# Attention and spectral mixing on one core: weight subtractions on GpSimd, earlier block loads, later rounding

## The chip, the cores and the metric

The kernel runs on one core of a Trainium2 chip. The metric is the device time of one execution in microseconds (us); lower is better. Engines are named as in the profile: PE is TensorE (PEld its weight loads), DVE is VectorE, ACT is ScalarE, POOL is GpSimd and SP is SyncE, which issues nearly all DMAs here.

## The reference

The input x has 2048 rows of 512. Two branches are mixed by a gate that each row computes for itself:

```python
x = A_x
g = _sigmoid((x * gate_w).sum(-1, keepdims=True))
a = _A_ref(x, A_wqkv, A_wo)      # attention, 32 heads of 16, softmax over 2048 keys, then @ wo
b = _B_ref(x, ...)               # y = Cr @ (x @ Wr.T) - Ci @ (x @ Wi.T): real part of a 2-D DFT
return g * a + (1 - g) * b
```

All of it is in 32-bit floats.

## The kernel before

**Matmuls in three passes.** TensorE multiplies a rounded type (F32R). To keep precision, each operand is split into a rounded part hi and a remainder lo = raw - hi. ScalarE makes hi by a copy with a change of type, and VectorE or GpSimd subtracts to make lo. A product is then hi x hi + hi x lo + lo x hi. The two halves of 64 rows run beside each other into two PSUM banks, so one pass is one pair of matmuls. This pair is the unit of the kernel's own calendar: `slots` counts pairs, and `beside()` is called after each.

**The calendar.** `after(n, f, ...)` puts a step into the instruction streams n slots from now. It sets only the place of the step in the order of its engine's queue. Each engine takes its queue in order, and an instruction that waits holds up all behind it on its engine.

**The stages.** In the first 680 us the kernel makes queries and keys (`project_t`, 12 slots each), values and the two DFT products of x (`project_s`, 12 slots each), and then the DFT along the sequence over blocks of 128 rows (48 slots each). Beside these it scans: matmuls of queries with keys, of which only the row maxima are kept (`scan`, and from a certain point `scan_folded`, which needs a ScalarE copy named fold and a VectorE maximum named fold or mx for each pair of chunks). How often a scan is placed between the pairs is set in slots (`scan_at`). After 680 us the attention itself follows, with exponentials on ScalarE.

**The steps that the change touches:**

- `project_t`: when a projection's 24 matmuls are done, ScalarE copies one bank to tx (one buffer), VectorE or GpSimd adds the other bank into s (three buffers), ScalarE rounds s into eh and GpSimd subtracts to make el; both are stored. The banks serve the projection after next.
- The weights of queries (wq) and keys (wk) come in two column halves, near and far. Splits of the far halves are placed by `after`: `split_w` is one ScalarE copy and one subtraction for each of the four row blocks d. The far halves of wq are first read by the projection that begins at slot 144.
- `project_s`: ScalarE copies one bank (tx, L545); the other is copied to ty (one buffer) or read directly; an add into va (values) or ab (DFT) follows on GpSimd or VectorE.
- `gate_sums` begins with the fourth block of the values. 16 blocks of x are loaded by SyncE into two buffers in turn, multiplied by the gate weights on GpSimd (`weigh`) and halved by adds (`add_up`); `gates` finishes the sum, and z, g = 1 / (1 + exp(-sum)) and gm = 1 - g follow. EVERY is 24 slots.
- `fold_keys`: key blocks are loaded, GpSimd subtracts one from another (fa), ScalarE rounds the difference (fh) and GpSimd makes the remainder; both are stored for later scans. It is called four times in the first DFT product.
- `renew`: in the DFT along the sequence the 16 right operands (second operands, b tiles) are exchanged when the cosine part is done. ScalarE rounds each, and four slots later GpSimd (odd) or VectorE (even) subtracts.

Of the kernel before, what the change touches and what calls it, by code (L numbers as in the profile page):

```python
# [10 lines left out]
F32 = mybir.dt.float32  # L11
F32R = mybir.dt.float32r
AF = mybir.ActivationFunctionType
ALU = mybir.AluOpType
# [10 lines left out]
NB = S // P  # L25
# [29 lines left out]
EVERY = 24  # L55
# [13 lines left out]
def build(tc, xT, xr, wqkv, wo, wrT, wiT, cr, ci, ct, gate, out):  # L69
    nc = tc.nc  # L70
    with ExitStack() as ctx:
# [25 lines left out]
        z = keep.tile([P, NB], F32, name="z")  # L97
        g = keep.tile([P, NB], F32, name="g")
        gm = keep.tile([P, NB], F32, name="gm")
# [103 lines left out]
        def halves_of(ps, lhs, rhs, first, last):  # L203

            for j in range(2):
                r = slice(64 * j, 64 * j + 64)
                nc.tensor.matmul(ps[j], lhs[r], rhs[r], start=first, stop=last)  # L207
# [65 lines left out]
        with ExitStack() as pf:  # L273
# [31 lines left out]
            def after(n, f, *args):  # L305

                count[0] += 1
                due.append((slots[0] + n, count[0], f, args))
# [21 lines left out]
            def beside():  # L330

                slots[0] += 1
                run_due()
                if pace[0] is None:
                    return
                since = slots[0] - spare[1] + 10
                pace[1] += 1.0 / (pace[0] if pace[0] != PART or since > 48 else CALM if since <= 8 else KEEN)
                while seen[0] < FRONT and pace[1] >= 1.0:
                    pace[1] -= 1.0
                    n = seen[0]  # L340
                    if n == FOLDED.start:
                        begin_folds()
                    if n in ROWS:
                        load_scan_beside(ROWS[n])
                    if n not in FOLDED:
                        scan(n, s1())
                        done = n
                    else:

                        scan_folded(n, 0, *beds)  # L350
                        done = behind(n - 1)
                    seen[0] += 1
                    if seen[0] == FRONT:
                        done = behind(n)
                    if done is not None and SEQ[done][1] == SCANS - 1:
                        for d, part in enumerate(shift(SEQ[done][0], nc.scalar.copy, nc.gpsimd.tensor_sub)):
                            maxima.append(part)
                            after((3, 8, 26, 31, 36)[d], part)
# [66 lines left out]
            with ExitStack() as px:  # L425
# [7 lines left out]
                def new_w():  # L433
                    ts = [wb.tile([P, ND, 512], F32R, tag=f"w{i}", name=f"w{i}") for i in range(2)]
                    return [[t[:, d, :] for d in range(ND)] for t in ts]

                def new_cw():

                    return list(zip(*(coefficients() for d in range(ND))))
# [14 lines left out]
                def fold_keys(f, g):  # L454

                    a, b = (ep.tile([P, 512], F32, tag="el", name="fa", bufs=4) for _ in range(2))
                    c = 2 * g
                    parts = [(a, b)]
                    if f:
                        for i, v in enumerate((a, b)):  # L460
                            nc.sync.dma_start(v, ks_d[f][:, (c + i) * 512:(c + i + 1) * 512])
                    else:

                        parts.append([rp.tile([P, 512], F32, tag="raw", name="fl") for _ in range(2)])
                        for n in range(2):
                            for i in range(2):
                                nc.sync.dma_start(parts[n][i], k_d[f][:, n, (c + i) * 512:(c + i + 1) * 512])
                        nc.sync.dma_start(kf_d[f][:, :, (c + 1) * 512:(c + 2) * 512],
                                          k_d[f][:, :, (c + 1) * 512:(c + 2) * 512])
                    hi = ep.tile([P, 512], F32R, tag="gb", name="fh", bufs=1)  # L470
                    lo = b.bitcast(F32R)

                    def store(i, v):
                        nc.sync.dma_start(kf_d[f][:, i, c * 512:(c + 1) * 512], v.bitcast(F32))

                    wait = 0 if f else 26
                    after(14 + wait // 2, nc.gpsimd.tensor_sub, a, a, b)
                    if wait:
                        after(33, nc.gpsimd.tensor_sub, parts[1][0], *parts[1])
                        after(39, nc.gpsimd.tensor_add, a, a, parts[1][0])  # L480
                    after(wait + 22, nc.scalar.copy, hi, a)
                    after(wait + 24, nc.gpsimd.tensor_sub, lo, a, hi.bitcast(F32))
                    after(wait + 28, store, 0, hi)
                    after(wait + 31, store, 1, lo)

                kept = []

# [66 lines left out]
                wq, wk = new_w(), new_cw()  # L554
                raws = [stk.tile([P, S], F32, tag="stk", name="raws") for _ in range(6)]
                q4 = [slice(d * 512, (d + 1) * 512) for d in range(4)]
                rq, rk = ([raws[4 + i][:, q4[d]] for d in range(ND)] for i in range(2))
                near, far = slice(0, 256), slice(256, 512)
# [24 lines left out]
                    split_w(wq, d, rq[d], cols=near)  # L583
                for d in range(ND):
                    after(1 + 2 * d, split_w, wk, d, rk[d], nc.vector, near)
                    after(84 + 5 * d, split_w, wq, d, rq[d], nc.vector, far)
                    after(130 + 12 * d, split_w, wk, d, rk[d], nc.vector, far)
                    for c in range(1, NC):
                        after(24 * c - 6 + 4 * d, split_x, d, c)
                def gate_sums():  # L590

                    work = stk.tile([P, 4, D], F32, tag="stk", name="gated")
                    sums_ = work[:, 3, :].rearrange("p (t k) -> p t k", k=32)
                    nc.sync.dma_start(work[:, 0, :], gate.to_broadcast([P, D]))

                    def load(t):
                        nc.sync.dma_start(work[:, 1 + t % 2, :], xr[t])

                    def weigh(t):
                        v = work[:, 1 + t % 2, :]  # L600
                        nc.gpsimd.tensor_mul(v, v, work[:, 0, :])

                    def add_up(t):
                        v = work[:, 1 + t % 2, :]
                        for n in (256, 128, 64):
                            nc.gpsimd.tensor_add(v[:, 0:n], v[:, 0:n], v[:, n:2 * n])
                        nc.gpsimd.tensor_add(sums_[:, t, :], v[:, 0:32], v[:, 32:64])

                    for t in range(NB):
                        after(EVERY * t, load, t)  # L610
                        after(EVERY * t + 22, weigh, t)
                        after(EVERY * t + 34, add_up, t)
                    after(EVERY * NB + 22, gates, sums_)

                def gates(sums_):
                    for n in (16, 8, 4, 2):
                        nc.gpsimd.tensor_add(sums_[:, :, 0:n], sums_[:, :, 0:n], sums_[:, :, n:2 * n])
                    nc.gpsimd.tensor_add(z, sums_[:, :, 0], sums_[:, :, 1])
                    after(10, lambda: nc.scalar.activation(z, z, AF.Exp, scale=-1.0))

                    def rest():
                        nc.vector.tensor_scalar_add(z, z, 1.0)
                        nc.vector.reciprocal(g, z)
                        nc.vector.tensor_scalar(gm, g, -1.0, 1.0, op0=ALU.mult, op1=ALU.add)

                    after(14, rest)

                order = [(wq, q_d, 0, 0), (wk, k_d, 0, 0), (wq, q_d, 1, 0)]
                order += [(w, dst, 0, c) for c in range(1, NC) for w, dst in ((wq, q_d), (wk, k_d))]
# [37 lines left out]
                for n, wait in enumerate((18, 78, 152, 202)):  # L667
                    after(wait, fold_keys, 2 * (n // 2), n % 2)
# [20 lines left out]
            with ExitStack() as py:  # L689
# [36 lines left out]
                for n, (ph, t, u) in enumerate(coef):  # L726
# [12 lines left out]
                    hi, lo = ready.pop(n)  # L739
# [25 lines left out]
                    for w in range(CS):  # L765
                        s = u * CS + w
                        for i, (c_, a_) in enumerate(((hi, ah[s]), (hi, al[s]), (lo, ah[s]))):
                            halves_of(pss[t], c_[:, w, :], a_, s == 0 and i == 0, s == NB - 1 and i == 2)
                            beside()
                            if n >= len(coef) - NU and 3 * s + i in AHEAD:  # L770
                                go_ahead(AHEAD.index(3 * s + i))
                        if swap:
                            if 3 <= s < 8:
                                early[s + 5] = load_operand(1, s + 5, cp)
                            after(1 + 5 * (s % 8) + 4 * (s // 8), renew, s)
                    if u == NU - 1:
                        tx = cp.tile([P, D], F32, tag="tx", name="tx")
                        last = n == len(coef) - 1
# [18 lines left out]
        with ExitStack() as pa:  # L797
# [143 lines left out]
            parts = []  # L941
# [435 lines left out]
```

## Time and profile before

| | us |
|---|---|
| median of 3 runs | 1709.04 |
| lowest and highest | 1708.09, 1710.79 |
| profiled execution | 1709.94 |
| its span, first to last instruction | 1708.0 |
| PE busy | 1691.4 |
| ACT busy | 1499.2 |
| DVE busy | 1189.2 |
| POOL busy | 818.9 |

Times in the views are us from the start of the span. A line of the order of time has start, duration, engine, line, operation, written tile <- read tiles, shapes, count, and in brackets the idle time just before it and what ended it. Lines such as L320 are shared by all steps that `after` or a helper places, so the names of the tiles tell which step it is. Busy time of PE is modelled from pipelined matmuls. PEclk is the granted clock as a share of the full one.

### The profile page before, as it was taken

The page shows a single profiled execution, that of the slowest core. Times are in us where ns is not written, and L with a number is a line of the kernel's source. Part 1 is how long each engine was busy: PE and PEld are TensorE (multiplying, and loading weights), DVE is VectorE, ACT ScalarE, POOL GpSimd, SP SyncE. Part 2 cuts the span into 40 slices and gives each one's busy share as a digit, 9 for nine tenths or more (in the row PEclk, how much of TensorE's full clock was granted, in tenths as well). Part 3 has the DMA queues.
Part 4 walks back from the last instruction along what each step waited for, and adds up shares of the span by engine and source line. Part 5 has one row for each costly group of instructions (what it writes and reads, how often), then busy time and mean ns, then how long its engine had stood idle before and what let it go on. Part 6 is the DMA issues. An engine that isn't in the chain of part 4 may idle for free.

```text
span 1708.0 us, 36306 instructions
## 1 busy us (share of the span) xinstructions
PE 1691.4 (99%) x13524; PEld 1036.1 (61%) x13524; DVE 1189.2 (70%) x2171; ACT 1499.2 (88%) x2470; POOL 818.9 (48%) x998
## 2 busy tenths in 40 slices
PE   9999999999999999999999999999999999999998
PEld 7898888889899895333333333333345555555554
DVE  5898888899999896666676666666742456653343
ACT  5447888888888888999999999999998888888886
POOL 3577676755556861434545455352323333334222
PEclk9999999999999999999999999999999999999999
DMA  7684668544448764355445445353426465575833
GB/s 263 237 286 116 215 200 223 168 120 126 119 126 216 195 136 95 100 138 133 134 115 123 109 127 141 82 148 63 101 67 145 139 149 151 135 187 139 196 90 127
DMA packets 151584, 251.18 MB, mean 147 GB/s; under 512 B 49792, under 2 KB 60528, under 8 KB 144112
## 3 DMA queue, kind: packets, MB, share of 16 engines
q1 hardware_dynamic: 136144, 227.49, 49.1%
q0 software_dynamic: 14688, 20.33, 5.1%
q8 instruction: 106, 1.74, 0.5%
q10 hardware_dynamic: 576, 1.05, 0.2%
q14 instruction: 70, 0.57, 0.1%
HBM read 168.56 MB, written 81.01 MB: 146 GB/s over the span
## 4 chain that ended last, share of the span: by engine, by line
PE 89%; DMA 2%; POOL 1%; DVE 1%; issue 1%; SPq 0%; ACT 0%; DVEq 0%; POOLq 0%; ACTq 0%
PE pvb L822 28%; PE xy L207 20%; PE s L232 19%; PE s L176 9%; PE s L207 8%; PE s L157 4%; DMA gated<-xr 1%; DVE fold L182 0%; DMA k_d<-eh 0%; DMA kf_d<-eh 0%; DVE y L937 0%; SPq L923 0%; DMA b<-o_d 0%; POOL va L648 0%; POOL el L320 0%
## 5 line engine op out<-in xcount | busy, mean ns | idle before, releaser
L256 ACT ACTIVATE eb<-s 128x1024 f32<-128x1024 f32 x512 | 579.3, 1132 | 60.2 <-PE s L232 60.1
L264 ACT ACTIVATE e<-s 128x512 f32<-128x512 f32 x1022 | 609.7, 710 | 0.0
L159 DVE TENSOR_REDUCE mx<-s 128x2 f32<-128x1024 f32 x380 | 460.9, 1224 | 195.7 <-PE s L157 195.5
L822 PE MATMUL pvb<-eb,va 128*17 128x512 f32 x2052 | 514.4, 597 | 0.0
L822 PE MATMUL pvb<-e,va 128*17 128x512 f32 x2044 | 513.5, 597 | 0.0
L182 DVE CUSTOM_DVE_ANT_0 fold<-s,fold 128x512 f32<-128x512 f32 x644 | 434.5, 690 | 53.1 <-PE s L176 29.4
L180 ACT ACTIVATE fold<-s 128x512 f32<-128x512 f32 x644 | 383.9, 602 | 66.3 <-PE s L176 37.7
L232 PEld LDWEIGHTS s<-qs,ks 50*128 50x128 f32 x2048 | 214.0, 184 | 361.6 <-ACT eb L256 268.7
L232 PE MATMUL s<-qs,ks 50*128 50x512 f32 x2048 | 424.3, 436 | 0.0
L207 PE MATMUL xy<-b,c 64*128 64x512 f32 x2448 | 382.6, 391 | 0.2 <-ACT c L376 0.2
L176 PE MATMUL s<-ks,qs 64*128 64x512 f32 x1288 | 283.8, 395 | 4.6 <-DVE mx L182 2.1
L207 PEld LDWEIGHTS xy<-b,c 64*128 64x128 f32 x2448 | 267.2, 184 | 23.5 <-ACT c L376 0.5
L822 PEld LDWEIGHTS pvb<-eb,va 128*17 128x17 f32 x2052 | 69.8, 96 | 189.5 <-issue 180.2
L176 PEld LDWEIGHTS s<-ks,qs 64*128 64x128 f32 x1288 | 149.5, 184 | 32.4 <-DVE mx L182 10.8
L157 PE MATMUL s<-ks,qs 48*128 48x512 f32 x760 | 160.3, 395 | 0.0
L841 POOL DMA_DIRECT2D r_d<-lc x31 | 18.0, 580 | 274.9 <-DVE lc L840 227.0
L207 PE MATMUL s<-b,b 64*128 64x512 f32 x1050 | 136.4, 390 | 0.2 <-DMA b<-o_d 0.2
L207 PE MATMUL xy<-w,b 64*128 64x512 f32 x768 | 116.6, 391 | 0.0
L834 POOL DMA_DIRECT2D lc<-ob x124 | 63.0, 515 | 109.6 <-DVE ob L831 104.6
L207 PEld LDWEIGHTS s<-b,b 64*128 64x128 f32 x1050 | 99.7, 185 | 24.1 <-issue 1.0
L408 POOL TENSOR_TENSOR c<-craw,c 128x512 fp32r<-128x512 f32 x84 | 109.9, 1309 | 6.7
L843 POOL DMA_DIRECT2D rb<-r_d x124 | 60.5, 495 | 96.1 <-DMA r_d<-lc 92.2
(147 smaller groups left out, 1624.8 us busy)
## 6 DMA issues: line engine op xcount, KB each, us to landing
qs<-q_d SPq DMA_DIRECT2D x90, 256.0 KB
craw<-cr SPq DMA_DIRECT2D x60, 256.0 KB
craw<-ct SPq DMA_DIRECT2D x48, 256.0 KB
ks<-k_d SPq DMA_DIRECT2D x46, 256.0 KB
ks<-kf_d SPq DMA_DIRECT2D x44, 256.0 KB
kept_None<-sum SPq DMA_DIRECT2D x40, 256.0 KB
craw<-kept_None SPq DMA_DIRECT2D x40, 256.0 KB
craw<-ci SPq DMA_DIRECT2D x32, 256.0 KB
```

The costliest lines, as they stand in the source:

```text
L157: nc.tensor.matmul(ps[:, j, :], qs[b:b + 48, qb * P:(qb + 1) * P], ks[b:b + 48, c * 512:(c + 1) * 512], start=True, stop=True)
L159: nc.vector.tensor_reduce(mx[p][:, :, qb, c], ps, axis=AX.X, op=ALU.max)
L176: nc.tensor.matmul(ps, qs[b:b + 64, qb * P:(qb + 1) * P], ks[b:b + 64, c * 512:(c + 1) * 512], start=True, stop=True)
L180: nc.scalar.activation(fold[j], ps, AF.Relu)
L182: nc.vector.tensor_tensor_reduce(out=fold[j], in0=ps, in1=fold[j], scale=1.0, scalar=-3.0e38, op0=ALU.add, op1=ALU.max, accum_out=mx[p][:, ...
L207: nc.tensor.matmul(ps[j], lhs[r], rhs[r], start=first, stop=last)
L232: nc.tensor.matmul(pss[j], ks[b:b + 50, kb * P:(kb + 1) * P], qs[b:b + 50, q0:q0 + 512], start=True, stop=True)
L256: nc.scalar.activation(e, ps, AF.Exp, scale=SCALE)
L264: nc.scalar.activation(e[j], pss[j], AF.Exp, scale=SCALE)
L408: sub(lo, raw, hi.bitcast(F32))
L822: nc.tensor.matmul(pvb[r:r + VC, :], va[:, kb, 2 * p + j, :], es[c][j], start=kb == 0, stop=kb == NB - 1, tile_position=(0, r))
L834: nc.gpsimd.dma_start(lc[32 * n:32 * n + 32, :], ob[r + DH:r + VC, :].rearrange("p (s e) -> p s e", e=16))
```

## The change

```diff
-                    after(wait + 22, nc.scalar.copy, hi, a)
-                    after(wait + 24, nc.gpsimd.tensor_sub, lo, a, hi.bitcast(F32))
-                    after(wait + 28, store, 0, hi)
-                    after(wait + 31, store, 1, lo)
+                    after(wait + 30, nc.scalar.copy, hi, a)
+                    after(wait + 32, nc.gpsimd.tensor_sub, lo, a, hi.bitcast(F32))
+                    after(wait + 36, store, 0, hi)
+                    after(wait + 40, store, 1, lo)
...
-                    after(84 + 5 * d, split_w, wq, d, rq[d], nc.vector, far)
+                    after(106 + 10 * d, split_w, wq, d, rq[d], nc.gpsimd, far)
...
-                        after(EVERY * t, load, t)
-                        after(EVERY * t + 22, weigh, t)
-                        after(EVERY * t + 34, add_up, t)
-                    after(EVERY * NB + 22, gates, sums_)
+                        at = EVERY * t + 40
+                        after(at - 35 if t > 1 else 0, load, t)
+                        after(at, weigh, t)
+                        after(at + 8, add_up, t, 256)
+                        after(at + 12, add_up, t, 128, 64, 32)
+                    after(EVERY * NB + 30, gates, sums_)
...
                     after(10, lambda: nc.scalar.activation(z, z, AF.Exp, scale=-1.0))
-                        nc.vector.tensor_scalar_add(z, z, 1.0)
-                        nc.vector.reciprocal(g, z)
-                        nc.vector.tensor_scalar(gm, g, -1.0, 1.0, op0=ALU.mult, op1=ALU.add)
-                    after(14, rest)
+                    after(16, nc.gpsimd.tensor_scalar_add, z, z, 1.0)
+                    after(24, nc.vector.reciprocal, g, z)
+                    after(30, lambda: nc.gpsimd.tensor_scalar(gm, g, -1.0, 1.0, op0=ALU.mult, op1=ALU.add))
...
-                            after(1 + 5 * (s % 8) + 4 * (s // 8), renew, s)
+                            after(1 + 5 * (s % 8) + 14 * (s // 8), renew, s)
```

1. `fold_keys`: the rounding fh comes 8 slots later, the remainder too, the stores 8 and 9 slots later.
2. The four splits of wq's far halves come at slots 106, 116, 126 and 136 instead of 84, 89, 94 and 99, with the subtraction on GpSimd instead of VectorE.
3. Block t of x is loaded at slot 24t + 5 from the third block on (24t before), multiplied at 24t + 40 (24t + 22), and its sum is taken in two pieces at 24t + 48 and 24t + 52 (24t + 34 in one). Its buffer was freed by the sum of block t - 2, now at 24t + 4, before at 24t - 14.
4. `gates` begins at slot 414 instead of 406. The addition of 1 and gm move to GpSimd; the reciprocal stays on VectorE, and the three come 16, 24 and 30 slots after the sums instead of 14 for all.
5. `renew` of operands 8 to 15 comes 10 slots later.

TensorE's instructions stay the same and in the same order. Line numbers behind the gate's functions fall by two.

VectorE in the projections, around 30 us of the profile. The w rows are the far halves of wq, b is a part of x, s the sums of a projection's two banks, and c a far half of wk:

```order
 L320 TENSOR_TENSOR s<-xy,tx 128x512
 L377 TENSOR_TENSOR b_236<-raws,b_235 128x512
-L377 TENSOR_TENSOR w_238<-raws,w_237 128x256 x2
 L320 TENSOR_TENSOR s<-s_544,tx 128x512
-L377 TENSOR_TENSOR w_238<-raws,w_237 128x256 x2
 L320 TENSOR_TENSOR s<-xy,tx 128x512 x3
 L377 TENSOR_TENSOR c<-raws,c 128x256
```

The four subtractions ahead of two adds are gone; the adds follow each other. On GpSimd the four now stand one by one between subtractions that make el.

ScalarE at the third call of `fold_keys`, around 231 us; tx and ty are copies of `project_s`, w a split of the next weights. Before:

```order
L376 CAST w_2701<-wraw 128x512
L180 ACTIVATE fold<-s 128x512 x2
L545 ACTIVATE tx<-xy 128x512
L180 ACTIVATE fold<-s 128x512 x2
L320 CAST fh<-fa 128x512
L180 ACTIVATE fold<-s 128x512 x3
L545 ACTIVATE tx<-xy 128x512
```

and now:

```order
L376 CAST w_2696<-wraw 128x512
L180 ACTIVATE fold<-s 128x512 x2
L545 ACTIVATE tx<-xy 128x512
L180 ACTIVATE fold<-s 128x512 x5
L545 ACTIVATE tx<-xy 128x512
L320 CAST fh<-fa 128x512
L180 ACTIVATE fold<-s 128x512 x4
```

The rounding fh stands three folds and one tx later.

More of the change, by code (lines that the diff above doesn't have):

```diff
@@ L601, in weigh, with add_up @@
                         nc.gpsimd.tensor_mul(v, v, work[:, 0, :])
-                    def add_up(t):
+                    def add_up(t, *parts):
                         v = work[:, 1 + t % 2, :]
-                        for n in (256, 128, 64):
-                            nc.gpsimd.tensor_add(v[:, 0:n], v[:, 0:n], v[:, n:2 * n])
-                        nc.gpsimd.tensor_add(sums_[:, t, :], v[:, 0:32], v[:, 32:64])
+                        for n in parts:
+                            dst = sums_[:, t, :] if n == 32 else v[:, 0:n]
+                            nc.gpsimd.tensor_add(dst, v[:, 0:n], v[:, n:2 * n])
                     for t in range(NB):
-                        after(EVERY * t, load, t)
-                        after(EVERY * t + 22, weigh, t)
-                        after(EVERY * t + 34, add_up, t)
-                    after(EVERY * NB + 22, gates, sums_)
+                        at = EVERY * t + 40
[4 more added lines that the diff above has]
+                    after(EVERY * NB + 30, gates, sums_)
                 def gates(sums_):
@@ L619, in gates @@
                     after(10, lambda: nc.scalar.activation(z, z, AF.Exp, scale=-1.0))
-                    def rest():
-                        nc.vector.tensor_scalar_add(z, z, 1.0)
-                        nc.vector.reciprocal(g, z)
-                        nc.vector.tensor_scalar(gm, g, -1.0, 1.0, op0=ALU.mult, op1=ALU.add)
-                    after(14, rest)
+                    after(16, nc.gpsimd.tensor_scalar_add, z, z, 1.0)
+                    after(24, nc.vector.reciprocal, g, z)
+                    after(30, lambda: nc.gpsimd.tensor_scalar(gm, g, -1.0, 1.0, op0=ALU.mult, op1=ALU.add))
                 order = [(wq, q_d, 0, 0), (wk, k_d, 0, 0), (wq, q_d, 1, 0)]
```

## The prediction

> **What bounds the kernel now.** I read the page's totals first, then the waits of TensorE, then its busy time in stretches of 10 us, and at each stretch that falls short the instructions in order of time.
>
> ```profile
> span 1708.0 us, 36306 instructions
> PE 1691.4 (99%) x13524; PEld 1036.1 (61%) x13524; DVE 1189.2 (70%) x2171; ACT 1499.2 (88%) x2470; POOL 818.9 (48%) x998
> PE s L176 <- DVE mx L182: 2.1, 6, 0.5
> PE s L176 <- ACT fold L180: 2.0, 2, 1.3
> PE xy L207 <- DVE s L320: 1.3, 1, 1.3
> PE xy L207 <- ACT tx L516: 0.6, 1, 0.6
> ```
>
> TensorE is busy 99% of the span, and the change leaves its instructions as they are, in number and order. So only two things can move the time: where TensorE stands still, and its clock. What it can win is a few microseconds of stalls; what it can lose is a new stall wherever a moved instruction is late. The four wait rows (total, times, longest) already name the places; the stretches date them:
>
> ```profile
> 120.00:130.00 10.00, 10.00 (x90) 9.81 (x88) 10.00 (x10) 2.85 (x7) 4.02 (x4) 1.00 1.04 344
> 130.00:140.00 10.00, 8.89 (x72) 7.00 (x70) 7.06 (x13) 5.43 (x11) 5.75 (x8) 1.00 0.29 84
> 230.00:240.00 10.00, 8.66 (x75) 7.39 (x74) 7.45 (x22) 7.35 (x14) 6.87 (x10) 1.00 0.65 200
> 260.00:270.00 10.00, 9.49 (x82) 7.79 (x80) 8.97 (x27) 8.64 (x19) 5.27 (x5) 1.00 0.47 142
> 550.00:560.00 10.00, 9.19 (x73) 6.79 (x73) 9.06 (x23) 8.54 (x17) 8.94 (x9) 1.00 0.72 185
> 37.00:41.00 4.00, 4.00 (x24) 0.57 0.65 248
> ```
>
> The columns are the stretch, its length, the busy time of PE, PEld, DVE, ACT and POOL, the granted clock, DMA share and GB/s (the last row, asked for PE alone, has PE's). An undisturbed stretch has 10.00 and some 90 matmuls. Short are 130 to 140 by 1.1 us, 230 to 240 by 1.3, 260 to 270 by 0.5, 550 to 560 by 0.8; and from 37 to 41 the granted clock is 0.57. Each lies where one edit works.
>
> **Far halves of the query weights (VectorE to GpSimd, later).** This is the largest term.
>
> ```profile
> 29.26 0.62 ACT L320 CAST eh<-s 128x512 fp32r<-128x512 f32 x1 [1.11 <-DVE s L320]
> 30.09 0.58 ACT L516 COPY tx<-s 128x512 f32<-128x512 f32 x1
> 30.22 1.65 DVE L377 TENSOR_TENSOR w<-raws,w 128x256 fp32r<-128x256 f32 x2 [0.39 <-ACT w L376]
> 30.45 2.90 PE L207 MATMUL xy<-b,c 64*128 64x512 f32 x24
> 31.80 0.68 DVE L320 TENSOR_TENSOR s<-s,tx 128x512 f32<-128x512 f32 x1
> 33.34 0.58 ACT L516 COPY tx<-xy 128x512 f32<-128x512 f32 x1
> 33.47 1.62 DVE L377 TENSOR_TENSOR w<-raws,w 128x256 fp32r<-128x256 f32 x2 [0.99 <-ACT w L376]
> 33.97 0.50 PE L207 MATMUL xy<-b,w 64*128 64x512 f32 x1 [0.62 <-ACT tx L516]
> 35.01 0.68 DVE L320 TENSOR_TENSOR s<-xy,tx 128x512 f32<-128x512 f32 x1
> 35.75 6.45 PE L207 MATMUL xy<-b,w 64*128 64x512 f32 x40 [1.28 <-DVE s L320]
> 42.98 0.59 ACT L516 COPY tx<-xy 128x512 f32<-128x512 f32 x1 [0.92 <-PE xy L207]
> 45.70 0.59 ACT L516 COPY tx<-xy 128x512 f32<-128x512 f32 x1 [0.40 <-PE xy L207]
> ```
>
> A projection's banks come free in two steps: ScalarE copies one (tx), VectorE adds the other (s). TensorE waits 0.62 us for a copy and 1.28 us for an add. Both are late because of the four subtractions: the copy at 30.09 is done at 30.67, but its add starts at 31.80, behind two of them (30.22 to 31.87); the next copy is done at 33.92 and its add starts at 35.01, behind the other two. tx has a single buffer, so a late add delays the next copy too.
>
> What it costs now: the group at 30.45 ends at 33.35. Two projections later, undisturbed, the copy would start 2 x 2.72 us on (45.70 less 42.98 is the period), at 38.8. It starts at 42.98, so 4.1 us are lost: 1.9 of named waiting, 0.5 for a lone matmul between them, and 4 us at clock 0.57, worth 1.7.
>
> Without the subtractions, and with their casts behind the copies in ScalarE's queue: cast eh ends at 29.88, copy to 30.5, add to 31.3 (0.68 each add, a little for each hand-over), cast to 31.9, copy to 32.5, add to 33.3. TensorE wants the bank at 33.2 to 33.35. What is late next is this same add, by 0.1 or 0.2 us. I take 3.9 us gained, of 4.1 at most; the other end is 0, if casts and copies still collide. With the idle time gone I expect the slow stretch gone; if it stays, 2.4 are gained.
>
> On GpSimd:
>
> ```profile
> L320 POOL TENSOR_TENSOR el<-s,eh 128x512 fp32r<-128x512 f32 x32 | 41.3, 1289 | 38.3 <-ACT eh L320 38.0 <-POOL el L320 0.2
> L377 DVE TENSOR_TENSOR w<-raws,w x8: 410/418/1317, 5.1 to 34.7; 128x256 fp32r<-128x256 f32 x8
> ```
>
> Half as wide as el, a subtraction there costs between half of 1.29 us and all of it; I take 0.7. One el and one subtraction per 2.72 us fit, since GpSimd waits 38.0 us for ScalarE around these el alone. The last is issued at slot 136 and first read at slot 155: 19 slots of 0.23 us (2.72 over 12) are 4.3 us for one cast and one subtraction. Cost: nothing, under that idle time; without it a late el would hold s buffers, at most 1.3 us.
>
> The second row shows that the same subtraction on VectorE took from 0.41 to 1.32 us. The Trainium skill (SBUF — State Buffer, "SBUF: two separate sides") says that GpSimd and VectorE share a port pair under an exclusive lock, which catches VectorE instructions with both inputs in SBUF; that speaks against moving work from one to the other. The spread agrees with it, but the adds that free the banks read one input from PSUM, and stand at 0.68 in both rows above. By that rule the four key-weight subtractions left on VectorE (same shape) would each pay up to 0.9 us, beside matmuls that do not read them yet; the sum stays.
>
> **x blocks 35 slots ahead.**
>
> ```profile
> 124.51 14.35 SPq L597 DMA_DIRECT2D gated<-xr  x3
> 134.01 1.30 POOL L601 TENSOR_TENSOR gated<-gated 128x512 f32<-128x512 f32 x1 [5.21 <-DMA gated<-xr]
> 136.59 0.60 ACT L320 ACTIVATE ty<-xy 128x512 f32<-128x512 f32 x1 [1.44 <-POOL va L648]
> 137.73 0.49 PE L176 MATMUL s<-ks,qs 64*128 64x512 f32 x1 [0.65 <-ACT fold L180]
> 126.34 0.60 ACT L545 ACTIVATE tx<-xy 128x512 f32<-128x512 f32 x1 [2.41 <-PE xy L207]
> 129.83 0.60 ACT L545 ACTIVATE tx<-xy 128x512 f32<-128x512 f32 x1 [2.40 <-PE xy L207]
> SPq L597 <- POOL gated L607: 34.1, 7, 12.4
> ```
>
> The first product waits 5.21 us on GpSimd for its block; the sum va queues behind it, ScalarE's ty waits 1.44 for va, its fold copy comes late, and TensorE waits 0.65. The block was issued at 124.51 and landed by 134.01. Twelve slots are 3.49 us (129.83 less 126.34); the product now stands at slot 40, some 11.6 us after the issue, against 9.5. So the chain goes: 0.65 gained. The rest of the 1.1 us there, 0.5, belongs to the begin of the folds and stays. Bounds: 1.1 gained, 0.5 lost.
>
> The new danger: a block's load stands one slot (0.3 us) behind the sum that frees its buffer, where 14 slots lay between. SyncE's queue will stand there, with row loads, fold loads and stores of ab behind it. The last row shows it standing there today for 34.1 us, 12.4 at once, while TensorE never waited for a row load. I price it at nothing; the cover is the loads' lead, and the third rival prices its loss.
>
> **Key differences rounded later.**
>
> ```profile
> 230.48 1.29 POOL L320 TENSOR_TENSOR fa<-fa 128x512 f32<-128x512 f32 x1
> 231.80 0.62 ACT L320 CAST fh<-fa 128x512 fp32r<-128x512 f32 x1 [1.83 <-POOL fa L320]
> 232.97 0.50 PE L176 MATMUL s<-ks,qs 64*128 64x512 f32 x2 [1.34 <-ACT fold L180]
> ```
>
> ScalarE stands 1.83 us at fh, because GpSimd reaches the difference late; the fold copies behind it are late and TensorE waits 1.34. Eight slots are 2.3 us, more than 1.83, so 1.3 gained; 0 if GpSimd's new order delays the difference as much. The stores go 8 or 9 slots later too, far ahead of the row loads that read them.
>
> **The gate's end.**
>
> ```profile
> 260.91 0.87 DVE L622 TENSOR_SCALAR z<-z 128x16 f32<-128x16 f32 x1
> 262.98 0.50 PE L176 MATMUL s<-ks,qs 64*128 64x512 f32 x2 [0.51 <-DVE mx L182]
> ```
>
> z, its reciprocal and gm sat on VectorE in one piece; two go to GpSimd and the reciprocal stands alone: 0.5 gained. But two waits are tighter: the exponential on ScalarE comes 10 slots after the gate's sums, which now begin only 2 slots behind the last block's sum, and the reciprocal waits for GpSimd's z with 8 slots in between. Behind them in their queues stand the fold copies and fold maxima that free TensorE's banks. Between 0 and the 1.3 us that the fh wait cost; I take 0.4, nearer to the small end since the slack is some 2 us. Net 0.1 gained.
>
> **Second operands from the eighth, 10 slots later.**
>
> ```profile
> 554.54 1.65 DVE L320 TENSOR_TENSOR b<-early,b 128x512 fp32r<-128x512 f32 x1
> 556.85 0.50 PE L176 MATMUL s<-ks,qs 64*128 64x512 f32 x2 [0.55 <-DVE mx L182]
> ```
>
> Two series of renewals, each every 8 slots, cross here. The 1.65 us that make the 0.55 belong to an early operand, which does not move; only the late ones stop crowding the queues behind it. I take 0.3 of the stretch's 0.8 gained, with 0.8 lost as the other end, if a late one meets GpSimd as this one did.
>
> **The sum.** 3.9 + 0.65 + 1.3 + 0.1 + 0.3 = 6.25 gained. Some twenty GpSimd instructions change places around va, ab and the fold differences; for collisions not seen in the trace I take 0.4 (between nothing and another 1.3). That leaves 5.85. The profiled execution took 1709.94 us around its span of 1708.0, so 1704.1 for one like it. It lies 0.9 above the median of 1709.04; the same gain from the median gives 1703.2. I take **1703.5**, between the two, a gain of 5.5.
>
> **The rivals.**
> *The slow stretch of the clock is not this stall's.* For: stalls of 1.34 and 0.65 us later had no slow stretch. Against: it starts some 1.5 us after the longest idle time. Then 1.7 less is gained: 1705.2. Chance 0.12. The Trainium skill (TensorE: Matmul & The Clock Gate, "Part 1: The HAM clock gate") has the clock halve after an idle window of about 3.4 us, watched in free-running windows; no wait here is that long, so by that rule this rival holds and the sum is 1.7 smaller, though the trace shows the drop after less.
> *The first stall stays in another form*, because ScalarE's queue of casts and copies, not VectorE, is the limit. For: its wait for tx is already there (0.62). Against: the schedule above, in which ScalarE has gaps. Then about 2 us are left: 1707.1. Chance 0.12.
> *Slower: SyncE stands at the x loads.* If it holds the reloads of first operands or fold loads past their due casts, ScalarE stands in order as it did at fh, 1.34 us of TensorE each time. Fourteen loads wait so. It decides from seven such stalls on, which eat the 5.85 and 3.4 more; with seven or eight the time is 1713. Against: the 34.1 us of such waiting now do no harm. Chance 0.09.
> *The waits only change places*, each moved step colliding as often as before: 1709. Chance 0.05.
>
> **How the numbers follow.** The forecast has 0.62. A measurement can tell 0.2%, about 3.4 us: the line is 1705.6. Above it the forecast's own bad ends (gate lost, operands lost) take little; the clock rival is mostly below it. Faster 0.69, same 0.22, slower 0.09. Low end: all stalls gone, 4.1 + 1.1 + 1.3 + 0.8 + 0.8 from the median is 1700.9, with the spread of the runs 1700.5. High end: past the second rival to 1708.6.
>
> **What would show it.** Right: no TensorE wait between 30 and 40 us and no clock below 1.00 there; ScalarE's fh without a wait; GpSimd's first product without a wait on its block; the reciprocal not in front of a TensorE wait. Wrong: the xy waits still at that place, ScalarE waiting on DMA for first operands, or SyncE's wait at the x loads above 34 us with a TensorE wait behind it.

## The result and the profile after

The changed kernel took 1704.2 us in the median of 10 runs (1701.33 to 1708.3), the kernel before 1708.99 on the same chip (1707.62 to 1711.26). The ratio is 0.9972, with an interval of [0.9963, 0.9982]: 4.8 us faster. The forecast was 1703.5. The profiled execution took 1704.42 around a span of 1702.5, against 1709.94 around 1708.0 before, so the two traces differ by 5.5 us.

The totals of the changed kernel:

```profile
span 1702.5 us, 36302 instructions
PE 1688.6 (99%) x13524; PEld 1044.7 (61%) x13524; DVE 1184.1 (70%) x2165; ACT 1498.8 (88%) x2470; POOL 823.2 (48%) x1004
```

and its waits of TensorE (total, times, longest):

```profile
PE s L157 <- DMA qs<-q_d: 1.6, 1, 1.6
PE s L176 <- DVE mx L182: 1.4, 4, 0.5
```

The waits for the projections' copies and adds and the 2.0 us for fold copies, all shown before, are gone. A wait that was not there stands on top: 1.6 us for rows of queries (qs) on DMA. The stretches that were short before (PE, PEld, DVE, ACT, POOL, clock, DMA share, GB/s) now read:

```profile
130.00:140.00 10.00, 9.54 (x83) 8.09 (x80) 7.70 (x16) 6.60 (x14) 7.35 (x9) 1.00 0.20 60
230.00:240.00 10.00, 10.00 (x90) 9.47 (x88) 8.53 (x26) 9.37 (x18) 9.13 (x13) 1.00 0.69 221
260.00:270.00 10.00, 10.00 (x90) 8.84 (x88) 8.75 (x27) 9.22 (x19) 5.49 (x6) 1.00 0.76 230
550.00:560.00 10.00, 9.45 (x82) 7.47 (x80) 8.86 (x23) 8.59 (x17) 9.38 (x9) 1.00 0.75 197
```

Two are full. The first keeps the 0.5 us that the prediction left to the begin of the folds, and the last is still short. Around the first stall I ask for PE alone:

```profile
37.00:41.00 4.00, 4.00 (x38) 1.00 0.61 210
53.00:56.00 3.00, 1.40 (x13) 1.00 0.90 327
56.00:60.00 4.00, 4.00 (x24) 0.57 0.03 12
```

The old place has a clock of 1.00 and 38 matmuls where it had 0.57 and 24. But 19 us later stands the same picture: idle time, and then four microseconds at 0.57 with 24 matmuls. The kernel before has a full row there:

```profile
53.00:56.00 3.00, 3.00 (x30) 1.00 0.97 315
```

**Where the time came from.** TensorE's order is the same in both, so a ScalarE copy of a projection's bank (tx) marks the same point of the work. Before, these stood at (start, duration, and idle time before them):

```profile
63.59 0.59 ACT L516 COPY tx<-xy 128x512 f32<-128x512 f32 x1 [1.91 <-PE s L157]
139.76 0.59 ACT L545 ACTIVATE tx<-xy 128x512 f32<-128x512 f32 x1
233.99 0.59 ACT L545 ACTIVATE tx<-xy 128x512 f32<-128x512 f32 x1
265.89 0.60 ACT L545 ACTIVATE tx<-xy 128x512 f32<-128x512 f32 x1
```

and the same copies now, with the one that the prediction showed at 42.98 ahead of them:

```profile
38.89 0.59 ACT L516 COPY tx<-xy 128x512 f32<-128x512 f32 x1 [0.38 <-PE xy L207]
62.91 0.59 ACT L516 COPY tx<-xy 128x512 f32<-128x512 f32 x1 [2.29 <-PE xy L207]
137.80 0.59 ACT L545 ACTIVATE tx<-xy 128x512 f32<-128x512 f32 x1
230.41 0.59 ACT L545 ACTIVATE tx<-xy 128x512 f32<-128x512 f32 x1
261.11 0.59 ACT L545 ACTIVATE tx<-xy 128x512 f32<-128x512 f32 x1
```

The differences are the lead of the changed kernel: 4.1 us, then only 0.7, then 2.0, 3.6 and 4.8; at the end of the span it is 5.5. So the first stall brought all of its 4.1 us and 3.4 of them were lost again within 24 us, while the later edits brought more than they were given.

**Where the 3.4 us went.** The order of time on TensorE and on SyncE's queue of the changed kernel:

```profile
49.38 0.32 SPq L119 DMA_DIRECT2D qs<-q_d  x1
52.92 0.40 PE L157 MATMUL s<-ks,qs 48*128 48x512 f32 x1
54.92 0.49 PE L157 MATMUL s<-ks,qs 48*128 48x512 f32 x1 [1.60 <-DMA qs<-q_d]
```

and before:

```profile
52.58 0.49 SPq L119 DMA_DIRECT2D qs<-q_d  x1
57.23 0.39 PE L157 MATMUL s<-ks,qs 48*128 48x512 f32 x1
```

These are the first scan's first two matmuls; of before the row is the second's. The rows of the queries are loaded beside the projections, one load every 7 slots, and `scan_at` starts the scan at a fixed slot. Before, the last of these loads was issued at 52.58 and the second matmul ran 4.7 us later without a wait. Now the load is issued at 49.38, 3.2 us earlier, and the scan's first matmul starts at 52.92; the second stands until 54.92, 5.5 us after the issue. By the lead of 4.1 us this matmul was due at 53.14, so it came 1.8 us late. Two things add up: the issue moved up by only 3.2 us, 0.9 less than the work that needs it, and the rows took 5.5 us where 4.7 had been enough before, another 0.9. The stall costs 1.6 us of idle time, and the slow stretch after it 1.7 (4 us at 0.57 of the clock): together the 3.4, to a tenth.

### The profile page after: what moved, and what is told of

Read it like the earlier page. It is cut to its first block, busy times and chain, and to the rows that moved or that the text cites. A ratio compares the mean times of both kernels' runs of the same rounds, so it can differ in the third digit from the quotient of the medians.

```text
span 1702.5 us, 36302 instructions
## 1 busy us (share of the span) xinstructions
PE 1688.6 (99%) x13524; PEld 1044.7 (61%) x13524; DVE 1184.1 (70%) x2165; ACT 1498.8 (88%) x2470; POOL 823.2 (48%) x1004
## 3 DMA queue, kind: packets, MB, share of 16 engines
q10 hardware_dynamic: 576, 1.05, 0.2%
## 4 chain that ended last, share of the span: by engine, by line
PE 92%; DVE 4%; DMA 3%; SPq 1%; issue 0%; POOL 0%; ACT 0%; DVEq 0%; POOLq 0%; ACTq 0%
PE pvb L820 29%; PE xy L207 23%; PE s L232 19%; PE s L176 9%; PE s L207 8%; PE s L157 5%; DVE mx L159 3%; DMA raws<-xT 1%; DMA q_d<-el 0%; DMA q_d<-eh 0%; DVE fold L182 0%; DMA qs<-q_d 0%; DVE y L935 0%; SPq L921 0%; DMA k_d<-eh 0%
## 5 line engine op out<-in xcount | busy, mean ns | idle before, releaser
L207 PE MATMUL xy<-b,c 64*128 64x512 f32 x2448 | 389.0, 391 | 0.1
L176 PE MATMUL s<-ks,qs 64*128 64x512 f32 x1288 | 293.1, 394 | 1.9 <-DVE mx L182 1.4
L207 PEld LDWEIGHTS xy<-b,c 64*128 64x128 f32 x2448 | 278.7, 185 | 16.1 <-ACT c L376 0.4
L176 PEld LDWEIGHTS s<-ks,qs 64*128 64x128 f32 x1288 | 157.5, 184 | 22.3 <-DVE mx L182 7.8
```

Source lines behind the costliest of these rows:

```text
L176: nc.tensor.matmul(ps, qs[b:b + 64, qb * P:(qb + 1) * P], ks[b:b + 64, c * 512:(c + 1) * 512], start=True, stop=True)
```

## The experiments

### One edit taken alone, one taken away

Only the far halves of the query weights:

```diff
 (kernel before)
-after(84 + 5 * d, split_w, wq, d, rq[d], nc.vector, far)
+after(106 + 10 * d, split_w, wq, d, rq[d], nc.gpsimd, far)
```

> Only the query weights' far halves are moved. Theory (the first stall's 4.1 us are won and 3.4 of them are given back when the first scan finds its query rows not landed, 1.6 us of waiting and a slow stretch of the clock): no TensorE wait between 30 and 40 us, a wait of about 1.6 us on the DMA of qs near 53 us, granted clock near 0.5 for some 3.4 us behind it, and a gain of about 0.7 us against the kernel before, 1708.3. Rival (the wait on qs is a chance of that one execution, or comes of the other edits): no such wait, 4.1 us gained, 1704.9.

It took 1707.93 us against 1709.1, ratio 0.9994 [0.9984, 1.0003]: no gain that can be told from nothing. Its wait of TensorE at the first scan:

```profile
PE s L157 <- DMA q_d<-eh: 1.2, 1, 1.2
```

and the stretches there, asked for PE alone:

```profile
50.00:55.00 5.00, 3.77 (x34) 1.00 1.03 326
55.00:60.00 5.00, 5.00 (x46) 1.00 0.23 88
```

The first stall is gone and the wait at the scan is there, 1.2 us; the profile names another DMA of the same queue for it, a store of queries. Here the clock held, so less was lost: the lead over before was 4.0 us at 39 us and 2.5 at 57.6. So this edit is enough to bring the wait. The profiled execution kept more of the lead (2.6 us at the end of the span) than the medians show (1.2).

All but that edit:

```diff
 (changed kernel)
-after(106 + 10 * d, split_w, wq, d, rq[d], nc.gpsimd, far)
+after(84 + 5 * d, split_w, wq, d, rq[d], nc.vector, far)
```

> The whole change but for the query weights' far halves. Theory (the other four edits carry 4.1 of the 4.8 us): 1704.9, the stall of 1.9 us and the slow clock between 33 and 41 us as before the change, and no wait on qs near 57 us. Rival (the gain is the first stall's, as the prediction had it): about 1708.

It took 1705.76 us, ratio 0.9978 [0.9968, 0.9987]. So the other edits bring 3.3 us, more than the 1.95 that the prediction's sum had for them (0.65 + 1.3 + 0.1 + 0.3, less 0.4). The first stall is there with the same two waits (1.3 and 0.6 us), but the slow stretch is not. PE alone:

```profile
33.00:37.00 4.00, 2.10 (x15) 1.00 0.36 139
37.00:41.00 4.00, 4.00 (x40) 1.00 0.68 259
```

and the copy that stood at 42.98 before:

```profile
41.21 0.59 ACT L516 COPY tx<-xy 128x512 f32<-128x512 f32 x1 [0.39 <-PE xy L207]
```

The same idle time, and 1.8 us less lost: the copy comes at 41.21. That had not been expected. The stall alone costs 2.3 us (41.21 less 38.89), and the slow stretch 1.8. There is no wait for the rows; their second matmul runs at 55.59, 4.6 us after the last issue at 51.03.

### The wait at the first scan

The theory was that the rows landing decide; with the scan later they have landed. A rival was that the DMA engines are full there, so that nothing but less traffic helps.

```diff
 (changed kernel)
-after(84, scan_at, PACE)
+after(100, scan_at, PACE)
```

> The changed kernel with the first scan 16 slots (3.7 us) later. Theory (the rows of the first scan are late against a TensorE that now comes 4.1 us earlier, and nothing else is wrong there): no wait on qs, clock 1.00 from 10 us on, 3.4 us less than the changed kernel, 1700.8. Rival (the slow stretch of the clock does not hang on waits): the wait is gone but a stretch at 0.5 stays somewhere below 70 us, 1702.5.

1701.0 us, ratio 0.995 [0.9936, 0.9965], in place of 0.9978 without the first edit. PE alone:

```profile
50.00:55.00 5.00, 5.00 (x48) 1.00 0.94 305
55.00:60.00 5.00, 5.00 (x46) 1.00 0.52 196
```

No wait, full clock, and the gain that the first edit had promised: 4.8 us between this kernel and the one without that edit (1705.76 less 1701.0), where 3.9 had been taken and each ratio is known to some 2 us.

The other way is to load earlier, the scan staying where it is:

```diff
 (changed kernel)
-after(7 * n, load)
+after((7 if p else 4) * n, load)
```

> The changed kernel with the eight row loads of the first scan issued 4 slots apart instead of 7, so the last one 21 slots (4.8 us) earlier in the queue. Theory (the last load is late because of its place in the queue): the wait on qs is gone, 3.4 us less than the changed kernel, 1700.8. Rival (the 16 DMA engines are full there and the bytes ahead of the last load decide): the last rows land as late as before, the wait stays at 1 us or more, 1704.

1702.53 us, ratio 0.9961 [0.9946, 0.9976]. On SyncE's queue, and on TensorE:

```profile
46.26 0.31 SPq L119 DMA_DIRECT2D qs<-q_d  x1
53.12 0.73 PE L157 MATMUL s<-ks,qs 48*128 48x512 f32 x2
```

The last load is issued 3.1 us earlier and the first scan's matmuls follow each other without a wait, although the DMA engines were as busy on the way there (a share of 1.05 from 44 to 50 us, 1.04 in the changed kernel). So the place of the issue decides, and in this trace the rival falls. The time alone does not tell the two apart: it is 1.7 us above the 1700.8 that the theory gave, and its interval, 1699.9 to 1705.0 by the 1709.1, holds that value and the rival's 1704.

Both together, and the later scan in the kernel before:

> The changed kernel with the first scan 16 slots later and the row loads 4 slots apart, both. Theory (either one alone takes the whole wait away): no wait on qs, and no more won than by the later scans alone, 1701.0 within 0.7 us. Rival (the rows still land late in some executions of the later scans): below 1700.

1701.97 us against 1709.98, ratio 0.9956 [0.9941, 0.9971]. No matmul waits for the rows, and nothing more is won than by the later scan alone, so either one is enough. The time is 1.0 us above the 1701.0, more than the 0.7 allowed; the interval, 1699.9 to 1705.0, holds the value.

```diff
 (kernel before)
-after(84, scan_at, PACE)
+after(100, scan_at, PACE)
```

> The kernel before with the first scan 16 slots later and nothing else. Theory (the rows are late only where TensorE comes to them without the 1.9 us and the slow clock of the first stall): the first stall stays; about 1 us is won in executions whose clock stays at 1.00, nothing in the others, so 0 to 1 us in the median, 1708 to 1709. Rival (the later begin of the scans is worth 3 us or more by itself, for example by taking load off VectorE, and the changed kernel's wait on its rows is beside the point): 1706 or less.

1709.51 us against 1709.98, ratio 0.9998 [0.9989, 1.0008]. In the kernel before, a later first scan by itself brings nothing that can be told; it keeps what the first edit wins. The later scan with the other four edits but without the first was not run.

### How large the wait is from run to run

The changed kernel again beside the one with the later scan, on one chip:

> The changed kernel once more, beside the next one on the same chip. Theory: 0.2 to 0.4% faster than the kernel before, a ratio of 0.997; a wait of some 1.5 us on qs near 53 us. Rival (the gain is of the first comparison's making): a ratio whose interval holds 1.

> The changed kernel with the first scan 16 slots later, once more. Theory: a ratio of 0.995, some 3 us less than the changed kernel beside it, with intervals that do not meet. Rival (the wait on qs costs only its own 1.6 us in most executions, since the clock mostly holds): 1.5 to 2 us less.

1702.8 us, ratio 0.9961 [0.9949, 0.9973], and 1700.88 us, ratio 0.9948 [0.9936, 0.996]. In this profiled execution of the changed kernel TensorE's wait for the rows was small, where it had been 1.6 us in the first:

```profile
PE s L157 <- DMA qs<-q_d: 0.4, 1, 0.4
```

and PE alone:

```profile
50.00:55.00 5.00, 4.61 (x40) 1.00 0.98 342
```

The clock held in the whole of this stretch and the next. The two kernels differ by 1.9 us, nearer to the rival's 1.5 to 2 than to the 3 of the theory that the slow stretch always follows; their intervals meet, so this pair alone doesn't prove a difference. The later scan is the fastest version seen. It beats the kernel before by 0.5% in both series, and against the changed kernel it was ahead in both (0.995 to 0.9972, 0.9948 to 0.9961).

### The other edits, one at a time

One execution of each, beside 1710.35 us of the kernel before on that chip. With so few runs the place in the trace decides, not the time.

```diff
 (kernel before: fold_keys alone)
-wait + 22, wait + 24, wait + 28, wait + 31
+wait + 30, wait + 32, wait + 36, wait + 40
```

> The kernel before with the key differences rounded 8 slots later and nothing else. Theory: ScalarE's wait of 1.83 us at fh is gone, TensorE has no wait between 230 and 240 us, and from there on the kernel is 1.3 to 1.6 us ahead of the kernel before, with nothing won or lost elsewhere by this edit. Rival (GpSimd reached the difference late because of the x blocks around it, so that the edit needs the other one): ScalarE still waits about 1 us at fh and TensorE 0.5 or more.

1707.79 us. PE alone:

```profile
30.00:40.00 10.00, 8.09 (x67) 1.00 0.50 187
230.00:240.00 10.00, 10.00 (x90) 1.00 0.75 248
```

and ScalarE's rounding in the order of time:

```profile
232.76 0.62 ACT L320 CAST fh<-fa 128x512 fp32r<-128x512 f32 x1
```

fh has no idle time before it, the stretch is full, and the lead over before went from 0.1 us at 205 to 1.7 at 234: 1.6 gained. This edit acts only there, so up to 200 us this is the kernel before. The first stall is there (8.09), at full clock. TensorE waits for the rows of the first scan here too, without the first edit:

```profile
PE s L157 <- DMA qs<-q_d: 1.0, 1, 1.0
```

Since the first stall came without its slow stretch, the scan was due earlier: the lead was 1.7 us at 41.29 and 0.4 at 59.69. So the rows' landing is close behind the first stall in the kernel before already.

```diff
 (kernel before: the loop over the blocks of x alone)
-after(EVERY * t, load, t) ... after(EVERY * NB + 22, gates, sums_)
+after(at - 35 if t > 1 else 0, load, t) ... after(EVERY * NB + 30, gates, sums_)
```

> The kernel before with the x blocks loaded and multiplied as in the changed kernel (the gate's sums 8 slots later with them) and z, g and gm as before. Theory: the 5.2 us of GpSimd at its first block shrink to about 1, the 0.65 us of TensorE at 137 us are gone, some 1.2 us won between 130 and 147 us, and SyncE stands about 54 us at the loads instead of 34 without a TensorE wait. The 0.5 us in front of the gate's reciprocal stay, a few us later. Rival (the standing SyncE holds up others): a TensorE wait on a DMA, or ScalarE waiting on one, and less than 0.5 us won.

1708.53 us. PE alone:

```profile
30.00:40.00 10.00, 8.09 (x55) 0.84 0.50 187
130.00:140.00 10.00, 9.55 (x80) 1.00 0.25 79
260.00:270.00 10.00, 9.24 (x80) 1.00 0.48 151
```

and a wait of SyncE's queue:

```profile
SPq L597 <- POOL gated L607: 50.9, 11, 14.1
```

From 130 us to the copy that before had at 139.76, the lead goes from 0.3 us to 1.3: 1.1 gained, where the changed kernel gained 1.3. SyncE stands 50.9 us at the loads, and the lead shows no loss behind it. At 260 to 270 this kernel is worse than before (9.24 against 9.49), and the lead is 1.1 us at 274 where it was 1.5 at 254. With this edit alone the gate's sums come 8 slots later while the piece of three VectorE instructions behind them stays whole; that this piece is the cause was not tried.

```diff
 (kernel before: the gate's end alone)
-after(14, rest)        # z + 1, reciprocal and gm, all on VectorE
+after(16, z + 1 on GpSimd); after(24, reciprocal); after(30, gm on GpSimd)
```

> The kernel before with the addition of 1 and gm on GpSimd and the reciprocal alone on VectorE, at the changed kernel's distances from the sums. Theory (the piece of 1.3 us on VectorE is what TensorE waited for): no TensorE wait between 260 and 266 us, 0.5 to 0.8 us won there. Rival (it is the shift by the later x blocks that takes the piece away from a full VectorE): a wait of 0.3 us or more stays there.

1707.62 us. PE alone:

```profile
260.00:270.00 10.00, 10.00 (x89) 1.00 0.49 151
```

The stretch is full, 0.8 us won (lead 1.1 to 1.9), and nothing waits for the new hand-overs.

```diff
 (kernel before: renewals alone)
-after(1 + 5 * (s % 8) + 4 * (s // 8), renew, s)
+after(1 + 5 * (s % 8) + 14 * (s // 8), renew, s)
```

> The kernel before with the second operands from the eighth on renewed 10 slots later and nothing else. Theory (the 1.65 us subtraction of an early operand makes the wait, and stays): the wait of about 0.5 us near 557 us stays, and between 0 and 0.4 us are won from 545 to 590 us. Rival (the crossing of the two series makes it): all 1.1 us of idle time between 550 and 570 us go.

1710.26 us. Two copies of a bank, ahead of the late renewals and behind all of them, stood before at

```profile
551.51 0.69 ACT L784 ACTIVATE tx<-xy,gm 128x512 f32<-128x512 f32 x1
609.23 0.68 ACT L784 ACTIVATE tx<-xy,gm 128x512 f32<-128x512 f32 x1
```

and here at

```profile
552.01 0.69 ACT L784 ACTIVATE tx<-xy,gm 128x512 f32<-128x512 f32 x1
609.49 0.68 ACT L784 ACTIVATE tx<-xy,gm 128x512 f32<-128x512 f32 x1
```

This kernel is 0.50 us behind at the first and 0.26 at the second: 0.24 gained, inside the 0 to 0.4 of the theory. Between the same two copies the changed kernel gains 0.29 and its repeat 0.28, the kernels without the first edit and with the earlier rows 0.26 and 0.27, and the four single edits that leave `renew` alone between -0.03 and 0.04. So the edit brings some 0.3 us, too little to show in the time of one execution. The wait of 0.55 us near 557 us stays, so the rival falls, and the row of 550 to 560 us is as short as before (9.21 against 9.19): the gain lies behind it. That this kernel came there 0.5 us late has nothing to do with the edit: near 138 us TensorE had waited 1.72 us for a fold copy, and before 0.65.

## Why the prediction was right, and which of its steps were not

The range and the sign held, and the total missed by 0.7 us, but the total came about otherwise than the sum said. The first term brought 3.2 us less than taken and the rest together 2.85 more, so that the total came close is luck. By the leads of the two profiled executions:

| term | taken | in the trace |
|---|---|---|
| first stall | 3.9 | 4.1 won, 3.4 lost at the first scan: 0.7 |
| x blocks | 0.65 | 1.3 |
| key rounding | 1.3 | 1.6 |
| gate's end | 0.1 | 0.8 |
| second operands | 0.3 | 0.3 |
| collisions not seen | -0.4 | none found |
| not attributed | | 0.4 at 250 us, 0.4 after 266 |
| sum | 5.85 | 5.5 |

**First stall: the mechanism right, "what is late next" wrong.** The adds follow the copies now (VectorE, TensorE and GpSimd in order of time):

```profile
30.48 0.69 DVE L320 TENSOR_TENSOR s<-s,tx 128x512 f32<-128x512 f32 x1 [0.64 <-ACT tx L516]
32.40 0.69 DVE L320 TENSOR_TENSOR s<-xy,tx 128x512 f32<-128x512 f32 x1 [1.23 <-ACT tx L516]
33.20 7.19 PE L207 MATMUL xy<-b,w 64*128 64x512 f32 x61
34.13 0.74 POOL L377 TENSOR_TENSOR w<-raws,w 128x256 fp32r<-128x256 f32 x1 [0.93 <-ACT w L376]
```

The second add is done at 33.09, and TensorE starts the group at 33.20: the 33.2 to 33.35 of the prediction. GpSimd's subtraction took 0.74 where 0.7 was taken. What failed is the sentence "What is late next is this same add, by 0.1 or 0.2 us". It looked at the chain that had been late, not at what else is due in the next 25 us by its own calendar. The rows of the first scan were next: in the trace of before their use came 4.7 us after the last issue, and I had not asked how much of that was spare. In the runs that waited they took 4.8 to 5.6 us, so in those nothing was spare: what TensorE gains ahead of the first scan beyond what SyncE's issue gains, it may lose there. That holds for the kernel before too: with the key rounding alone and with the gate's end alone, neither of which has acted by then, 1.3 and 1.2 us of lead were lost there after a first stall at full clock.

**The first rival (slow stretch) was partly true.** The same stall, 1.9 us idle in two pieces, had a slow stretch in before and in two single edits (0.84 in the row of the x blocks alone above, 0.77 from 37 to 41 us with the renewals alone), and none in four other executions that kept it. So its price is 2.3 or 4.1 us by the execution, and 4.1 was the dear end; the prediction's 2.4 for the stall alone agrees with the 2.3. The profile of before was one with it, which the prediction could not see from a single trace.

**x blocks.** "GpSimd's first product without a wait on its block" was wrong:

```profile
132.77 1.29 POOL L601 TENSOR_TENSOR gated<-gated 128x512 f32<-128x512 f32 x1 [1.17 <-DMA gated<-xr]
```

and SyncE's queue stands at the loads for

```profile
SPq L597 <- POOL gated L607: 54.2, 11, 14.2
```

The product waits 1.17 us in place of 5.21, and the chain behind it goes all the same. TensorE's idle time in the stretch fell by 0.65 (9.54 less 8.89), as taken. The lead rose by 1.3 because the named wait is not all that a stall costs. The rows show it in the count of matmuls: 72 before and 83 now, 11 more, at 0.111 us each (10 us over 90) 1.2 us. At 230 to 240 it is 75 and 90, 1.7 us, where the lead rose 1.6 and the wait was 1.34; at 260 to 270 it is 82 and 90, 0.9 us, where the lead rose 0.8 and the wait was 0.51. So these three terms were too small for one reason in common: I costed them by idle time, which leaves out that TensorE issues fewer matmuls per busy microsecond around a wait. In the gate's end the 0.4 set aside for new waits comes on top.

The stall itself changes from run to run, and in step with its cause. With the old loads GpSimd waited 4.8, 5.2, 5.4, 5.5 and 6.3 us for its first block in five executions, and TensorE 0.2, 0.7, 0.8, 0.8 and 1.7 us for the fold copy; with the new loads and the same scan it was 1.2 to 2.7 us in five, and TensorE never waited for the fold copy. So the chain of the prediction is right, and the 0.65 of one trace was one value out of a wide spread.

**The third rival (SyncE at the x loads) falls.** The row above is the 34.1 us of before risen to 54.2, as its condition asked, and no TensorE or ScalarE wait on a load of first operands stands behind it. The rows that TensorE did wait for were issued at 49.38, long before these loads.

**Key rounding and gate's end.** The difference is still late on GpSimd, but ScalarE comes to it later:

```profile
228.30 1.30 POOL L320 TENSOR_TENSOR fa<-fa 128x512 f32<-128x512 f32 x1 [1.71 <-DMA fa<-ks_d]
230.88 0.62 ACT L320 CAST fh<-fa 128x512 fp32r<-128x512 f32 x1
262.87 0.25 DVE L320 RECIPROCAL g<-z 128x16 f32<-128x16 f32 x1
```

1.28 us lie between the end of fa and the rounding. The reciprocal (the last row, on VectorE) stands without a wait, so the 0.4 us put down for new waits there were not needed.

**Second operands.** The term held. Between the copies at 551.51 and 609.23 us of before, the lead of the changed kernel goes from 4.90 to 5.19 us: 0.29, where 0.3 was taken, and 0.24 with this edit alone. The named waits do not show it: the wait for the VectorE maxima is 1.2 us in 540 to 570 against 1.1 before. The early operand's 1.65 us still make one of 0.55, as the prediction said. Which instruction the late operands no longer hold up was not followed.

## What to carry to other kernels

When a stall goes, everything behind it comes forward by its length, except what is paced by DMAs: list the next loads that have a slot of their own, with the time from the last issue to the first use, and compare it with the time gained. Size a stall by the matmuls that are missing from its stretch, not by its named idle time. A slow stretch of the clock that follows a stall in one profile may be missing in the next, so cost it once with and once without.

## What the runs showed of the hardware

**The clock.** The granted clock fell after 1.9 us of idle time in two pieces in 3 of 7 executions that had this very stall (the kernel before, two single edits) and not in the other 4; at the first scan it fell after 1.6 us once, and not after waits of 0.4, 0.9, 1.0 and 1.2. Each time it was one stretch of 3.4 us at half the clock (in the rows above, 4 us at 0.57), worth 1.7 to 1.8 us. Length alone does not decide: two single waits of 1.7 us, for fold copies near 138 us (renewals alone) and 231 us (the kernel before with the later scan), left the clock at 1.00. The Trainium skill (TensorE: Matmul & The Clock Gate, "Part 1: The HAM clock gate (the "warmup" mystery)") says that the activity window is free-running, which agrees with a drop that the same stall brings only sometimes. Its threshold, an idle window of about 3.4 us, does not agree: here 1.6 to 1.9 us of idle time were sometimes enough. Where in the window a stall must fall was not tried.

**Rows from DRAM under load.** With the DMA engines 0.9 to 1.0 busy, the last load of query rows was usable 5.5 us after its issue in one execution of the changed kernel (49.38 to 54.92) and 4.8 in the next (48.74 to 53.54); in three single edits that waited it was 5.3 to 5.6. The kernel before used them after 4.7 without a wait, and the kernel without the first edit after 4.6. So the same load at the same place of the program took between at most 4.6 and 5.6 us, a spread of 1.0 where the first scan's longest wait was 1.6.

**VectorE beside GpSimd.** The two durations of a 128x256 subtraction on VectorE, which the prediction showed as 0.41 to 1.32 us, have a plain pattern. In the first 55 us of the trace of before, ten ran with nothing on GpSimd and took 0.41 to 0.42 us each. Six began while GpSimd was making an el; they took 1.29 to 1.32 us, and each ended 0.3 us after that el. The adds that free the banks, with one input from PSUM, took 0.68 to 0.69 us beside an el or not. Two of the four subtractions that made the first stall were among the six, which is 1.8 us of VectorE's time in front of the two late adds. Of the four key-weight subtractions left on VectorE three still take 1.31 us in the changed kernel, and no matmul waits for them, as the prediction said.
